# An attention turn written out in another order, with the identity matrix built by VectorE

## The chip, the cores and the metric

One core of a Trainium2 chip runs the whole program. The metric is the device time of one execution in microseconds, and a kernel is compared by the median of its runs. Names of engines here: TensorE (PE in the rows; PEld is its weight load), VectorE (DVE), ScalarE (ACT), GpSimd (POOL), and SyncE (SP), whose queue issues nearly all DMAs.

## What is computed

Attention with a random-feature kernel over 4 batches, 8 heads, 576 positions of 64 elements, with 128 features; its output goes through two MLPs (512 to 2048 to 512) on 2304 rows. Queries, keys, values are fp32; the MLP weights come in as fp64.

```python
def phi(x):
    proj = np.einsum('bhsd,df->bhsf', x, w_phi)
    proj = proj - np.max(np.abs(proj), axis=-1, keepdims=True)
    return np.concatenate([np.exp(proj), np.exp(-proj)], axis=-1)
q_p, k_p = (phi(q), phi(k))
kv = np.einsum('bhsf,bhsd->bhfd', k_p, v)
z = np.sum(k_p, axis=2)
num = np.einsum('bhsf,bhfd->bhsd', q_p, kv)
den = np.einsum('bhsf,bhf->bhs', q_p, z)[..., None] + 1e-06
return (num / den).astype(np.float32)
...
h = x @ w_in                      # first MLP
g = np.maximum(0.01 * h, h)
x = (g @ w_out).astype(np.float32)
...
h = x @ w_in                      # second MLP
sp = np.where(h > 20.0, h, np.log1p(np.exp(np.minimum(h, 20.0))))
out = ((h * np.tanh(sp)) @ w_out).astype(np.float32)
```

## The kernel before

The work is cut into 16 pairs (a batch and two heads). Of 576 positions, 512 are the main part (four blocks of 128) and 64 are left over; the leftovers of two neighbouring pairs are projected together, so `k_proj_left` comes in every other turn.

Nothing schedules the instructions: inside `manual_schedule` each engine runs them in the order in which the Python code issues them, and semaphores do the rest. `start()` prepares pairs 0 and 1. Then the loop over `attention(n)` runs n = 0 to 16, one **turn** each, with three pairs in hand: the sums and numerators of w = n, the projections of p = n + 1, the transposes of t = n + 2, and the loads of t + 1.

The steps of a turn are these. `transposes` turns keys and queries on TensorE with the identity matrix; `split` (L76 to L78) evicts them as a high part on ScalarE (`kth`, `qth`, `lh`) and a low part on VectorE (`ktl`, `qtl`, `ll`). `q_left` casts the leftover queries into place (L286). `q_proj` (four calls) and `k_proj` (two) project with three matmuls for each product (`three`, L81 to L83); `k_guard` subtracts the maximum from the keys' projections (`mx` L290, `kd` L291), while queries are copied by ScalarE (`qd`, L328), reduced over partitions by POOL (`qm`, L330, one call for each head) and guarded by VectorE in `q_guard` (L335). `exp` (L313) makes `qp` and `kp` for both signs. `kv(i, c)` sums key features times values for head h and sign a (c = 2h + a), `L353` copies the sums from PSUM, `nd` multiplies queries with them (L373, L365) and divides (L377 to L386), and `x_t` transposes the result into `X` one turn later (L395 to L399).

`Conv` turns fp64 weights into fp32: a unit is clamped (L147), shifted (L149), rescaled on ScalarE (L150), its sign and low bits taken (`e`, L156) and joined (`c`, L128); a unit that is kept in SBUF is then split by `split_w` into `wh` (ScalarE, L166) and `wl` (VectorE, L167). `conv0` has 10 units of the kind split and then 5 of the kind store, one for each of turns 1 to 15; each `step` finishes the unit opened a turn earlier and opens the next. Its data come through `Conv.load`, on SP's queue.

PSUM has four banks for the ring `a` (transposes, projections) and four for `b` (sums, numerators, x). After the turns, `moe(g)` runs the two MLPs; its first two steps already stand in turns 14 and 15. The identity comes from the library's `make_identity` (L194), a memset and a select on POOL. In turns 8 to 11, `window(0, ...)` splits a part of `X` behind the turn.

The order of a turn before, in its own lines:

```python
            if has_w:
                q_guard(w)
            if has_p:
                q_proj(p, 0)
                k_proj(p, 0)
                q_proj(p, 1)
            if has_w:
                if w:
                    kv(w, 0)
                q_exp(1)
            if has_p:
                q_proj(p, 2)
                k_proj(p, 1)
            if has_w:
                q_exp(-1)
            if has_p:
                q_proj(p, 3)
                if p % 2 == 0:
                    k_proj_left(p)
```

Of the kernel before, what the change touches and what calls it, by code (L numbers as in the profile page):

```python
# [24 lines left out]
def attention_two_mlps_kernel(  # L25
# [12 lines left out]
    nc = tc.nc  # L38
# [51 lines left out]
    class Conv:  # L90
# [5 lines left out]
        def __init__(self, which, units):  # L96
            self.which, self.units, self.at, self.loaded = which, units, 0, 0
            self.stage, self.open = {}, None
# [19 lines left out]
        def done(self):  # L118
            return self.at == len(self.units) and self.open is None

# [69 lines left out]

    with tc.manual_schedule():
        nc.scalar.preload_act_table_set("natural_log_exp_and_others")
        ident = ap.tile([P, P], F32, name="ident", bufs=1)
        make_identity(nc, ident)  # L194
        wbd = ap.tile([P, 2, F], F32, name="wbd", bufs=1)
        nc.vector.memset(wbd, 0.0)
        nc.vector.memset(two, 2.0)
# [20 lines left out]
        def load(i):  # L218
            b, p = divmod(i, NP)
# [8 lines left out]
            if i % 2 == 0:  # L228
# [9 lines left out]
            vm = s["vm"] = vmain[i % NV]  # L238
            nc.sync.dma_start(
                out=vm[:, :, 0:NM, :].rearrange("p h t d -> p h (t d)"),  # L240
                in_=v[b, h0:h0 + 2, 0:MAIN, :].rearrange("h (p t) d -> p h (t d)", t=NM),
            )
            vl = s["vl"] = vleft[i % NV]
            for r in range(2):
                nc.sync.dma_start(out=vl[r * LEFT:(r + 1) * LEFT, r, 0:D], in_=v[b, h0 + r, MAIN:S, :])
# [3 lines left out]
        load(0)  # L249
        load(1)  # L250
# [86 lines left out]
        def kv(i, c):  # L337
            s, l = st[i], lf[i // 2]
            h, a = divmod(c, 2)
            if c == 0:  # L340
                s["kvp"] = bank("b")
            o = s["kvp"][:, c * P:(c + 1) * P]

            for t in range(NM):
                nc.tensor.matmul(out=o, lhsT=s["kp"][a][:, h, t, :], rhs=s["vm"][:, h, t:NM + 1:NM - t, :],  # L345
                                 start=(c == 0 and t == 0), stop=False, skip_group_check=True)
            if c == 3:
                both = s["kvp"].rearrange("p (h a n) -> p h a n", h=2, a=2)
                for x in range(2):
                    nc.tensor.matmul(out=both[:, :, x, 0:D + 1], lhsT=l["lp"][x][:, i % 2, :], rhs=s["vl"],  # L350
                                     start=False, stop=(x == 1), skip_group_check=True)
                s["kv"] = ap.tile([P, 4, P], F32, tag="kv", name="kv", bufs=1)
                nc.scalar.activation(out=s["kv"], in_=s["kvp"].rearrange("p (c n) -> p c n", n=P), func=AF.Copy)  # L353

        def nd(i, c):
            s = st[i]
            t = bank("b")
            if c == 0:
                s["xn"] = ap.tile([P, NM, 2, D], F32, tag="xn", name="xn")
            if c == 2:  # L360

                g = t[:, 0:2 * (D + 1)].rearrange("p (c n) -> p c n", n=D + 1)
                kv_ = s["kv"].rearrange("p (h a) n -> p h a n", a=2)
                for a in range(2):
                    nc.tensor.matmul(out=g, lhsT=s["qp"][a].rearrange("p h n -> p (h n)")[:, MAIN:MAIN + P], rhs=kv_[:, :, a, 0:D + 1],  # L365
                                     start=(a == 0), stop=(a == 1))
                ng = 2
            else:
                g = t.rearrange("p (c n) -> p c n", n=P)
                for j, u in enumerate(range(2 * c, 2 * c + 2)):  # L370
                    for h in range(2):
                        for a in range(2):
                            nc.tensor.matmul(out=g[:, 2 * j + h, 0:D + 1], lhsT=s["qp"][a][:, h, Q_COL[h][u]:Q_COL[h][u] + P],  # L373
                                             rhs=s["kv"][:, 2 * h + a, 0:D + 1], start=(a == 0), stop=(a == 1))
                ng = 4
            den = ap.tile([P, 4], F32, tag="den", name="den")[:, 0:ng]
            nc.vector.tensor_scalar(out=den, in0=g[:, :, D], scalar1=1e-6, scalar2=None, op0=ALU.add)  # L377
            nc.vector.reciprocal(out=den, in_=den)
            if c == 2:
                s["xl"], s["lb"] = xleft[i % 2], t  # L380
                for h in range(2):
                    r = slice(h * LEFT, (h + 1) * LEFT)
                    nc.vector.tensor_scalar(out=s["xl"][r, h], in0=g[r, h, 0:D], scalar1=den[r, h:h + 1], scalar2=None,
                                            op0=ALU.mult)
            else:
                nc.vector.tensor_tensor(  # L386
                    out=s["xn"][:, 2 * c:2 * c + 2].rearrange("p a h d -> p (a h) d"), in0=g[:, :, 0:D],
                    in1=den.unsqueeze(2).to_broadcast([P, ng, D]), op=ALU.mult)

        def x_t(i):  # L390
# [6 lines left out]
            o = s["lb"][:, 2 * P:2 * P + LEFT]  # L397
# [4 lines left out]
        def k_exp(i):  # L402
            if i % 2 == 0:
                lf[i // 2]["lp"] = [exp(lf[i // 2]["kd"], "lp", sg) for sg in (1, -1)]
            st[i]["kp"] = [exp(st[i]["kd"], "kp", sg) for sg in (1, -1)]

        def start():
# [12 lines left out]
            kp_head(0, 1)  # L420
# [3 lines left out]
            k_proj_left(0)  # L424
            transposes(1, "k")
# [3 lines left out]
            kp_head(1, 0)  # L429
            kp_head(1, 1)  # L430
            kv(0, 0)
            kv(0, 1)
            load(2)

        def attention(n):
# [4 lines left out]

            def q_exp(sg):
                if sg == 1:
                    st[w]["qp"] = []
# [279 lines left out]
```

## Time and profile before

| what | value |
|---|---|
| median of 3 runs | 1033.09 us (1032.63 to 1036.21) |
| profiled execution, its own time | 1029.51 us |
| its span, first to last instruction | 1027.7 us |
| TensorE busy | 1001.1 us (97%) |
| VectorE, ScalarE, POOL busy | 753.2, 501.3, 72.6 us |
| chain of work that ended last | PE 92%, DVE 5%, issue 1%, ACT 1% |
| DMA | 72.84 MB, mean 71 GB/s |

The profile is of one execution; its own time is the span and 1.8 us around it, and 3.6 us below the median of the runs. Busy time adds up what instructions took. A matmul that follows another overlaps with it, so its row begins before the row ahead ends; the distance between two starts says how fast TensorE really goes. `x4` merges four neighbours, and a bracket at the end of a row gives the idle time just ahead on that engine and what ended it. A waiting instruction of an engine holds everything behind it on that engine.

### The profile page before, as it was taken

To read this page: it belongs to the slowest core of one execution; us is meant where nothing else is said; L and a number is where in the kernel's file an instruction comes from. 1 tells how busy PE (TensorE), PEld (TensorE's weight loads), DVE (VectorE), ACT (ScalarE), POOL (GpSimd) and SP (SyncE) were. 2 spreads that over 40 slices of the span, in tenths; PEclk is the share of its full clock that TensorE was granted. 3 is DMA by queue.
4 is the path that set the end of the run, shared out by engine and by line. 5 is a ranking of instruction groups with operands and counts; after the bars stand their busy time and mean duration, and the time that the engine had idled before them with its cause. 6 is when DMAs were issued, how large, how long until landed. Compare 5 with 4: busy or idle time off the path is not lost.

```text
span 1027.7 us, 14556 instructions
## 1 busy us (share of the span) xinstructions
PE 1001.1 (97%) x5544; PEld 871.2 (85%) x5544; DVE 753.2 (73%) x1389; ACT 501.3 (49%) x839; POOL 72.6 (7%) x38
## 2 busy tenths in 40 slices
PE   6999999999999999999999999999999999999998
PEld 5999988998888888998888888888888988888886
DVE  5888898876995666666533546978876888868976
ACT  4666666654554333343333445545544555545543
POOL 3322333220000000000000000000000000000000
PEclk9999999999999999999999999999999999999999
DMA  4333323313541344444311221000100100001001
GB/s 130 111 111 111 100 82 93 121 43 113 160 148 42 123 144 154 134 144 136 110 62 31 93 82 62 1 1 0 41 1 1 41 1 21 1 1 41 1 1 42
DMA packets 55494, 72.84 MB, mean 71 GB/s; under 512 B 10496, under 2 KB 39808, under 8 KB 55424
## 3 DMA queue, kind: packets, MB, share of 16 engines
q1 hardware_dynamic: 55264, 71.84, 21.6%
q8 instruction: 44, 0.72, 0.3%
q14 instruction: 26, 0.21, 0.1%
q10 hardware_dynamic: 160, 0.07, 0.0%
HBM read 57.48 MB, written 14.42 MB: 70 GB/s over the span
## 4 chain that ended last, share of the span: by engine, by line
PE 92%; DVE 5%; issue 1%; ACT 1%; POOL 0%; ACTq 0%; DVEq 0%; POOLq 0%
PE a L81 14%; PE a L82 14%; PE a L83 14%; PE b L82 13%; PE b L81 13%; PE b L83 13%; PE b L373 6%; PE b L345 4%; DVE qd L335 1%; PE a L266 1%; DVE kd L291 1%; DVE mx L290 1%; ACT kv L353 1%; PE b L395 1%; PE b L350 1%
## 5 line engine op out<-in xcount | busy, mean ns | idle before, releaser
L81 PE MATMUL a<-wh,wh 128*128 128x512 f32 (+1 forms) x640 | 235.6, 368 | 0.0
L82 PE MATMUL a<-wl,wh 128*128 128x512 f32 (+1 forms) x640 | 235.4, 368 | 0.0
L83 PE MATMUL a<-wh,wl 128*128 128x512 f32 (+1 forms) x640 | 235.4, 368 | 0.0
L81 PEld LDWEIGHTS a<-wh,wh 128*128 128x128 f32 x640 | 120.6, 188 | 20.2
L82 PEld LDWEIGHTS a<-wl,wh 128*128 128x128 f32 x640 | 120.7, 189 | 20.1
L83 PEld LDWEIGHTS a<-wh,wl 128*128 128x128 f32 x640 | 120.6, 188 | 20.0
L571 DVE TENSOR_TENSOR gl<-g,gh 128x512 fp32r<-128x512 f32 x72 | 49.9, 693 | 110.1 <-ACT gh L568 110.1
L82 PE MATMUL b<-gl,wh 128*128 128x512 f32 (+1 forms) x320 | 117.7, 368 | 0.0
L81 PE MATMUL b<-gh,wh 128*128 128x512 f32 (+1 forms) x320 | 117.7, 368 | 0.0
L83 PE MATMUL b<-gh,wl 128*128 128x512 f32 (+1 forms) x320 | 117.7, 368 | 0.0
L82 PE MATMUL b<-wl,gh 128*128 128x512 f32 x288 | 112.1, 389 | 0.0
L81 PE MATMUL b<-wh,gh 128*128 128x512 f32 x288 | 112.1, 389 | 0.0
L83 PE MATMUL b<-wh,gl 128*128 128x512 f32 x288 | 112.1, 389 | 0.0
L568 ACT ACTIVATE gh<-g 128x512 fp32r<-128x512 f32 x72 | 45.5, 632 | 115.9 <-PE b L83 109.4
L330 POOL PARTITION_ALL_REDUCE qm<-qd x32 | 71.9, 2249 | 140.7 <-DVE qd L335 122.1
L593 ACT ACTIVATE gh<-u 128x512 fp32r<-128x512 f32 x72 | 45.6, 633 | 70.6 <-PE b L82 63.9
L567 DVE TENSOR_TENSOR g<-g,a 128x512 f32<-128x512 f32 x72 | 49.4, 686 | 38.0 <-ACT g L564 35.2
L150 ACT ACTIVATE c<-c 128x512 f32<-128x512 f32 x64 | 40.3, 630 | 68.5 <-DVE c L147 68.3
L373 PE MATMUL b<-kv,qp 128*128 128x65 f32 x512 | 62.7, 276 | 7.5 <-ACT kv L353 7.5
L620 ACT ACTIVATE r<-e,two 128x512 f32<-128x512 f32 x72 | 51.7, 718 | 36.3 <-DVE e L605 36.3
L83 PEld LDWEIGHTS b<-gh,wl 128*128 128x128 f32 x320 | 60.3, 189 | 10.1
L81 PEld LDWEIGHTS b<-gh,wh 128*128 128x128 f32 x320 | 60.4, 189 | 10.0
(103 smaller groups left out, 1773.7 us busy)
## 6 DMA issues: line engine op xcount, KB each, us to landing
stage<-in_moe_w_in_dram SPq DMA_DIRECT2D x32, 512.0 KB, 3.6
stage<-in_moe_w_out_dram SPq DMA_DIRECT2D x32, 512.0 KB, 3.5
scr<-c SPq DMA_DIRECT2D x37, 256.0 KB, 2.0
wstage<-scr SPq DMA_DIRECT2D x32, 256.0 KB, 3.8
kn<-in_k_dram SPq DMA_DIRECT2D x16, 256.0 KB, 3.8
qn<-in_q_dram SPq DMA_DIRECT2D x16, 256.0 KB, 4.0
vmain<-in_v_dram SPq DMA_DIRECT2D x16, 256.0 KB, 3.2
out_dram<-X SPq DMA_DIRECT2D x16, 256.0 KB, 2.2
```

The source lines that it names most:

```text
L81: nc.tensor.matmul(out=o, lhsT=wh_, rhs=xh, start=start, stop=False)
L82: nc.tensor.matmul(out=o, lhsT=wh_, rhs=xl, start=False, stop=False)
L83: nc.tensor.matmul(out=o, lhsT=wl_, rhs=xh, start=False, stop=stop)
L150: nc.scalar.activation(out=c, in_=c, func=AF.Copy, scale=2.0 ** -112)
L330: nc.gpsimd.partition_all_reduce(s["qm"][:, h, :], s["qd"][:, h, :], P, bass_isa.ReduceOp.absmax)
L345: nc.tensor.matmul(out=o, lhsT=s["kp"][a][:, h, t, :], rhs=s["vm"][:, h, t:NM + 1:NM - t, :], start=(c == 0 and t == 0), stop=False, skip_ ...
L373: nc.tensor.matmul(out=g[:, 2 * j + h, 0:D + 1], lhsT=s["qp"][a][:, h, Q_COL[h][u]:Q_COL[h][u] + P], rhs=s["kv"][:, 2 * h + a, 0:D + 1], s ...
L567: nc.vector.tensor_tensor(out=g, in0=g, in1=h, op=ALU.max)
L568: nc.scalar.activation(out=hi, in_=g, func=AF.Copy)
L571: nc.vector.tensor_tensor(out=lo, in0=g, in1=hi.bitcast(F32), op=ALU.subtract)
L593: nc.scalar.activation(out=hi2, in_=u2, func=AF.Copy)
L620: nc.scalar.activation(out=r0, in_=e0, func=AF.Ln, bias=two)
```

## The change

The identity is built on VectorE by eight small instructions (`identity`): a running count 1 to 32 along a row, its 32 x 32 transpose, and four comparisons. `load` issues keys and queries at the head of a turn and returns a function that issues the values, which is called after the sums. A turn begins with all four query projections, then both query exponentials, then the key projections; the sums are made by sign (`kv(i, a)`, both heads and the leftovers), so that the exponential of the next pair's first sign stands between them; `q_guard(p)` stands in the turn that projected p. `x_t` comes ahead of the numerators. `nd` uses two PSUM banks instead of three, with six divisors in the second. `conv0.step` becomes `begin`, ahead of the transposes, and `join`, between the numerators; the low half `wl` of a unit follows at the next `begin`.

```diff
+        def begin(self):
+            self.load(1)
+            if self.rest is not None:
+                self.rest()
...
+            nc.vector.tensor_scalar(out=c, in0=hw.bitcast(F32), scalar1=F64_TOP, scalar2=-F64_TOP,
+                                    op0=ALU.min, op1=ALU.max)
+            nc.vector.tensor_scalar(out=lw, in0=lw, scalar1=29, scalar2=None, op0=ALU.logical_shift_right)
+            self.open = (u, kind, c, hw, lw)
+            return lambda: nc.scalar.activation(out=c, in_=c, func=AF.Copy, scale=2.0 ** -112)
+        def join(self):
...
+            nc.vector.scalar_tensor_tensor(out=e, in0=hw, scalar=-(1 << 31), in1=lw,
+                                           op0=ALU.bitwise_and, op1=ALU.bitwise_or)
+            self.load(1)
+            nc.vector.scalar_tensor_tensor(out=c.bitcast(I32), in0=c.bitcast(I32), scalar=3, in1=e,
+                                           op0=ALU.logical_shift_left, op1=ALU.bitwise_or)
+            if kind == "store":
...
+            else:
+                self.rest = split_w(self.which, u // 2, u % 2, c)
...
+    def identity(out):
+        Q = 32
+        one, row, col = (ap.tile([P, Q], F32, name=x, bufs=1) for x in ("one", "row", "col"))
+        nc.vector.memset(one, 1.0)
+        nc.vector.memset(out, 0.0)
+        nc.vector.tensor_tensor_scan(out=row, data0=one, data1=one, initial=0.0, op0=ALU.mult, op1=ALU.add)
+        nc.vector.transpose(out=col, in_=row)
+        for r in range(0, P, Q):
+            nc.vector.tensor_tensor(out=out[r:r + Q, r:r + Q], in0=row[r:r + Q], in1=col[r:r + Q], op=ALU.is_equal)
...
-        make_identity(nc, ident)
...
+        identity(ident)
...
-        def kv(i, c):
+        def kv(i, a):
...
+            for h in range(2):
+                for t in range(NM):
+                    nc.tensor.matmul(out=both[:, h, a, :], lhsT=s["kp"][a][:, h, t, :], rhs=s["vm"][:, h, t:NM + 1:NM - t, :],
+                                     start=(a == 0 and h == 0 and t == 0), stop=False, skip_group_check=True)
+            nc.tensor.matmul(out=both[:, :, a, 0:D + 1], lhsT=l["lp"][a][:, i % 2, :], rhs=s["vl"],
+                             start=False, stop=(a == 1), skip_group_check=True)
...
             kp_head(0, 0)
-            kp_head(0, 1)
             k_proj(0, 1)
...
             k_proj_left(0)
+            kp_head(1, 0)
             transposes(1, "k")
...
-            kp_head(1, 0)
+            kp_head(0, 1)
             kp_head(1, 1)
+            q_guard(0)
             kv(0, 0)
-            kv(0, 1)
-            load(2)
+            load(2)()
...
+            values = load(t + 1) if t + 1 < PAIRS else lambda: None
+            if has_p:
+                for c in range(4):
+                    q_proj(p, c)
             if has_w:
-                q_guard(w)
+                st[w]["qp"] = [exp(st[w]["qd"], "qp", sg) for sg in (1, -1)]
...
+                for c in range(2):
+                    k_proj(p, c)
+                if p % 2 == 0:
+                    k_proj_left(p)
...
                 if w:
                     kv(w, 0)
...
+                if has_p:
+                    k_exp(p, 0)
+                kv(w, 1)
+                kv_copy(w)
+            values()
             if has_p:
...
+                q_guard(p)
+            rebase = conv0.begin() if n >= CONV0 else lambda: None
             if has_t:
                 transposes(t)
                 q_left(t)
             elif has_w:
                 moe(n - (PAIRS - 2))
+            rebase()
             if has_p:
-                k_exp(p)
-            if has_w:
-                nd(w, 0)
+                k_exp(p, 1)
             if 0 <= w - 1:
                 x_t(w - 1)
             if has_w:
+                nd(w, 0)
+            conv0.join()
+            if has_w:
                 nd(w, 1)
-                nd(w, 2)
-            if t + 1 < PAIRS:
-                load(t + 1)
```

Where instructions stand, at the three places of which the prediction speaks. First TensorE from a turn's last sums to its end, before (`vmain`, `vleft` are the values, `kn`, `qn` keys and queries to be transposed, `xn` the divided result of the pair ahead):

```order
L345 MATMUL b<-vmain_89,kp 128x128 x12
L350 MATMUL b<-vleft_92,lp 128x2x65 x2
L266 MATMUL a<-ident,kn 128x128 x4
L266 MATMUL a<-ident,qn 128x128 x4
L373 MATMUL b<-kv,qp 128x65 x8
L395 MATMUL b<-ident,xn 128x128 x4
L398 MATMUL b<-fold,xleft_94 128x64
L373 MATMUL b<-kv,qp 128x65 x8
L365 MATMUL b<-kv,qp 128x130 x2
```

and now:

```order
L398 MATMUL b<-vmain_96,kp 128x128 x8
L400 MATMUL b<-vleft_99,lp 128x2x65
L398 MATMUL b<-vmain_96,kp 128x128 x8
L400 MATMUL b<-vleft_99,lp 128x2x65
L318 MATMUL a<-ident,kn 128x128 x4
L318 MATMUL a<-ident,qn 128x128 x4
L445 MATMUL b<-ident,xn 128x128 x4
L448 MATMUL b<-fold,xleft_101 128x64
L419 MATMUL b<-kv,qp 128x65 x16
L425 MATMUL b<-kv,qp 128x130 x2
```

The transposes of `xn` and the leftovers' fold moved ahead of the first numerators, which are now in one run with the second; the sums of a pair stand together.

Second, ScalarE from the head of a turn, before (`qd` the query copies, `wh` and `c` of the conversion, `kv` the copy of the sums):

```order
L328 ACTIVATE qd<-a 128x320
L328 ACTIVATE qd<-a 128x256
L313 ACTIVATE qp<-qd 128x1152
L328 ACTIVATE qd<-a 128x256
L313 ACTIVATE qp<-qd 128x1152
L328 ACTIVATE qd<-a 128x320
L166 ACTIVATE wh_975<-c 128x512
L150 ACTIVATE c<-c 128x512
L353 ACTIVATE kv<-b 128x512
L77 ACTIVATE kth<-a 128x512
L77 ACTIVATE qth<-a 128x2x256
```

and now, from the end of one turn into the next:

```order
L137 ACTIVATE c<-c 128x512
L365 ACTIVATE kp<-kd 128x1024
L446 ACTIVATE X<-b 128x512
L202 ACTIVATE wh_564<-c 128x512
L380 ACTIVATE qd<-a 128x320
L380 ACTIVATE qd<-a 128x256 x2
L380 ACTIVATE qd<-a 128x320
L365 ACTIVATE qp<-qd 128x1152 x2
L365 ACTIVATE lp<-kdl 128x256
L365 ACTIVATE kp<-kd 128x1024
L406 ACTIVATE kv<-b 128x512
```

The copy `wh` of a conversion unit moved from the middle of the next turn to the end of its own, directly ahead of the next turn's query copies, and the rescaling `c` from ahead of the `kv` copy to behind the evictions.

Third, SP's queue from the loads of pair 3 to those of pair 4, before (`stage` is a conversion unit's data):

```order
L224 DMA kn<-in_k_dram 128x2x256
L224 DMA qn<-in_q_dram 128x2x256
L239 DMA vmain_88<-in_v_dram 128x2x256
L245 DMA vleft_91<-in_v_dram 64x64 x2
L115 DMA stage<-in_moe_w_in_dram 128x4x256
L115 DMA stage<-in_moe_w_out_dram 128x1024
L115 DMA stage<-in_moe_w_in_dram 128x4x256
L224 DMA kn<-in_k_dram 128x2x256
L224 DMA qn<-in_q_dram 128x2x256
L234 DMA kl<-in_k_dram 64x2x64 x2
L234 DMA ql<-in_q_dram 64x2x64 x2
```

and now:

```order
L272 DMA kn<-in_k_dram 128x2x256
L272 DMA qn<-in_q_dram 128x2x256
L289 DMA vmain_95<-in_v_dram 128x2x256
L295 DMA vleft_98<-in_v_dram 64x64 x2
L272 DMA kn<-in_k_dram 128x2x256
L272 DMA qn<-in_q_dram 128x2x256
L282 DMA kl<-in_k_dram 64x2x64 x2
L282 DMA ql<-in_q_dram 64x2x64 x2
L289 DMA vmain_96<-in_v_dram 128x2x256
L295 DMA vleft_99<-in_v_dram 64x64 x2
L114 DMA stage<-in_moe_w_in_dram 128x4x256
L114 DMA stage<-in_moe_w_out_dram 128x1024
```

The first two `stage` loads moved from ahead of all of pair 4's loads to behind its last values.

## Rows read from the trace of the kernel before

**Rows 1.** The page's part 1: busy us (share of the span) xinstructions.

```profile
PE 1001.1 (97%) x5544; PEld 871.2 (85%) x5544; DVE 753.2 (73%) x1389; ACT 501.3 (49%) x839; POOL 72.6 (7%) x38
```

**Rows 2.** Stretches: their length, then busy us of each engine, clock, DMA.

```profile
113.00:127.20 14.20, 13.40 (x115) 12.93 (x114) 12.06 (x27) 9.34 (x16) 4.28 (x2) 1.00 0.35 113
127.20:140.90 13.70, 13.06 (x114) 12.82 (x113) 12.41 (x26) 9.52 (x16) 4.76 (x2) 1.00 0.30 92
450.00:1027.00 577.00, 573.15 (x2641) 478.89 (x2639) 410.09 (x687) 265.12 (x435) 0.00 (x0) 1.00 0.11 38
```

**Rows 3.** TensorE's waits to 260 us: waiter, releaser, total us, times, longest.

```profile
PE a L266 <- POOL ident masks.py:199: 9.2, 1, 9.2
PE b L373 <- ACT kv L353: 7.5, 12, 1.2
```

**Rows 4.** Timeline, TensorE, turns 7 and 8: start, us, instruction, idle before.

```profile
113.02 0.39 PE L81 MATMUL a<-qth,wbh 128*128 128x320 f32 x1
117.58 0.35 PE L81 MATMUL a<-wbh,lh 128*128 128x256 f32 x1 [0.38 <-DVE kd L291]
122.60 2.00 PE L373 MATMUL b<-kv,qp 128*128 128x65 f32 x16 [0.42 <-ACT kv L353]
127.25 0.39 PE L81 MATMUL a<-qth,wbh 128*128 128x320 f32 x1
136.28 2.00 PE L373 MATMUL b<-kv,qp 128*128 128x65 f32 x16 [0.64 <-ACT kv L353]
140.94 0.39 PE L81 MATMUL a<-qth,wbh 128*128 128x320 f32 x1
```

**Rows 5.** Timeline of TensorE: first query matmul of turns 1 and 14.

```profile
29.91 0.39 PE L81 MATMUL a<-qth,wbh 128*128 128x320 f32 x1
...
213.19 0.39 PE L81 MATMUL a<-qth,wbh 128*128 128x320 f32 x1
```

**Rows 6.** Timeline of POOL and TensorE to the start of turn 0.

```profile
8.86 0.28 POOL masks.py:199 TENSOR_SCALAR_AFFINE_SELECT ident<-ident 128x128 f32<-128x128 f32 x1 [7.93 <-issue]
9.20 1.11 PE L266 MATMUL a<-ident,kn 128*128 128x128 f32 x4 [9.20 <-POOL ident masks.py:199]
13.10 0.39 PE L81 MATMUL a<-qth,wbh 128*128 128x320 f32 x1 [0.34 <-DVE qtl L286]
15.03 4.30 POOL L330 PARTITION_ALL_REDUCE qm<-qd  x2 [5.89 <-ACT qd L328]
16.42 0.62 PE L266 MATMUL a<-ident,qn 128*128 128x128 f32 x4
19.52 0.39 PE L81 MATMUL a<-qth,wbh 128*128 128x320 f32 x1 [0.70 <-DVE qtl L286]
```

**Rows 7.** SP's queue; DMA issues to 4.6 us, KB, us to landing.

```profile
3.31 1.25 SPq L234 DMA_DIRECT2D ql<-in_q_dram  x2
...
kn<-in_k_dram SPq DMA_DIRECT2D x1, 256.0 KB, 2.7
...
ql<-in_q_dram SPq DMA_DIRECT2D x2, 32.0 KB, 2.1
```

**Rows 8.** Timeline of SP's queue, and DMA issues from 26.0 to 26.5 us.

```profile
24.62 0.37 SPq L239 DMA_DIRECT2D vmain<-in_v_dram  x1
26.24 0.58 SPq L115 DMA_DIRECT2D stage<-in_moe_w_in_dram  x1
...
stage<-in_moe_w_in_dram SPq DMA_DIRECT2D x1, 512.0 KB, 3.8
```

**Rows 9.** Timeline of POOL and VectorE in turns 7 and 8.

```profile
118.92 2.14 POOL L330 PARTITION_ALL_REDUCE qm<-qd  x1 [0.69 <-ACT qd L328]
120.68 0.65 DVE L147 TENSOR_SCALAR c<-stage 128x512 f32<-128x512 f32 x1
133.14 2.62 POOL L330 PARTITION_ALL_REDUCE qm<-qd  x1 [0.69 <-ACT qd L328]
133.50 1.52 DVE L147 TENSOR_SCALAR c<-stage 128x512 f32<-128x512 f32 x1
```

More of the change, by code (lines that the diff above doesn't have):

```diff
@@ L97, in __init__ @@
             self.which, self.units, self.at, self.loaded = which, units, 0, 0
-            self.stage, self.open = {}, None
+            self.stage, self.open, self.rest = {}, None, None
         def load(self, ahead):
@@ L237, in load, with values @@
                         )
[L238 to L245, printed above, removed]
+            def values():
+                vm = s["vm"] = vmain[i % NV]
+                nc.sync.dma_start(
+                    out=vm[:, :, 0:NM, :].rearrange("p h t d -> p h (t d)"),
+                    in_=v[b, h0:h0 + 2, 0:MAIN, :].rearrange("h (p t) d -> p h (t d)", t=NM),
+                )
+                vl = s["vl"] = vleft[i % NV]
+                for r in range(2):
+                    nc.sync.dma_start(out=vl[r * LEFT:(r + 1) * LEFT, r, 0:D], in_=v[b, h0 + r, MAIN:S, :])
+            return values
         for r in range(2):
             nc.scalar.dma_start(out=wbd[r * D:(r + 1) * D, r, :], in_=w_phi)
-        load(0)
-        load(1)
+        load(0)()
+        load(1)()
         wbh = ap.tile([P, 2 * F], F32R, name="wbh", bufs=1)
@@ L335, in q_guard, with kv_copy @@
             nc.vector.tensor_tensor(out=s["qd"], in0=s["qd"], in1=s["qm"], op=ALU.subtract)
-        def kv(i, c):
+        def kv(i, a):
             s, l = st[i], lf[i // 2]
-            h, a = divmod(c, 2)
-            if c == 0:
+            if a == 0:
                 s["kvp"] = bank("b")
[L342 to L353, printed above, removed]
+            both = s["kvp"].rearrange("p (h a n) -> p h a n", h=2, a=2)
+            for h in range(2):
[4 more added lines that the diff above has]
+                             start=False, stop=(a == 1), skip_group_check=True)
+        def kv_copy(i):
+            s = st[i]
+            s["kv"] = ap.tile([P, 4, P], F32, tag="kv", name="kv", bufs=1)
+            nc.scalar.activation(out=s["kv"], in_=s["kvp"].rearrange("p (c n) -> p c n", n=P), func=AF.Copy)
         def nd(i, c):
@@ L454, in attention @@
                     kv(w, 0)
-                q_exp(1)
-            if has_p:
-                q_proj(p, 2)
-                k_proj(p, 1)
-            if has_w:
-                q_exp(-1)
-            if has_p:
-                q_proj(p, 3)
-                if p % 2 == 0:
-                    k_proj_left(p)
-            if n >= CONV0 and not conv0.done():
-                conv0.step()
-            if has_w:
-                for c in range(1 if w else 2, 4):
-                    kv(w, c)
+                if has_p:
[3 more added lines that the diff above has]
+            values()
+            if has_p:
+                q_guard(p)
+            rebase = conv0.begin() if n >= CONV0 else lambda: None
             if has_t:
```

71 lines of the change are left out of this document (37 added, 34 removed).

## The prediction

> **What bounds the kernel now.** I went from the page to stages, then to single turns. The page first: TensorE is busy for 1001.1 of 1027.7 us [rows 1], so at most 26.6 us of the span are open to any reordering; what can move must be TensorE idle. By stage, the last 577 us hold only 3.9 us of it [rows 2]; the diff leaves that part's instruction order alone, so it can only start earlier. The idle time is at the start and in the attention turns, and the waits say for what: 9.2 us for the identity matrix that POOL builds, 7.5 us in 12 waits for ScalarE's copy of the sums `kv` [rows 3], and a smaller wait at the leftover key projection.
>
> Next, two neighbouring turns by starts of TensorE [rows 4]. Turn 7 lasts from 113.02 to 127.25, 14.23 us. The leftover key projection would have followed the last query projection at 117.04, but starts at 117.58: 0.54 lost to `kd`. The numerator's first matmul would follow the transposes at 122.02 and starts at 122.60: 0.58 lost to `kv`. Turn 8 lasts 13.69 us; its numerator starts at 136.28 instead of 135.48: 0.80 lost. Without these waits the turns are 13.11 and 12.89 us. Turns 1 to 13 run from 29.91 to 213.19 [rows 5], 183.3 us; seven of the long and six of the short kind without waits would be 169.1, so **14.2 us** is what the turns can give. The busy rows give less: the two windows show 0.80 and 0.64 us idle [rows 2], over thirteen turns 9.4. I take the starts, as a matmul after a wait has its fill counted as busy. The Trainium skill (Trainium Kernel Development and Optimization, Performance Expectations) also calls matmul busy time a bad metric because matmuls are pipelined; by the busy rows the sum below would be 8.6 us, by the starts 13.4, and which is right the changed profile will tell.
>
> **The change part by part.**
>
> *Identity.* POOL's select ends at 9.14 and TensorE begins at 9.20 [rows 6]; the keys `kn` were issued at 0.72 and take 2.7 us [rows 7], so they lie there from 3.4 on. VectorE's eight new small instructions appear in no row; bounded by a 0.06 us memset and the 0.42 us of a 128x256 operation they are 0.5 to 3.4 us, and I take 1.2, as most are as small as the memsets. Begun at about 1.1 they end at 2.3, before the keys; the other memsets that they push back end by 4.4, before anything needs them. The next limit is then the leftover queries: the last `ql` is issued at 3.93 and takes 2.1 [rows 7], so the leftover transposes end at about 6.1 instead of 11.2. From there to the first query projection the chain of splits and casts takes 1.9 us, so 8.0 instead of 13.10 [rows 6]: 5.1 gained. In `start` one half of the key exponentials now waits for the second `kd` ahead of the eviction of pair 1's keys: about 0.5 lost. Turn 0 begins near 15.0 instead of 19.52: **4.5 gained**. POOL loads code ahead of its reductions; before, this was hidden in the 5.9 us between the select and the first reduction [rows 6], now it may take what the select waited for (7.9 us), ending near 9, when the first reduction is due at 9.9. If both waits add up it ends at 13.8 and turn 0 gets some 2.5 longer.
>
> *Turn order.* TensorE now does four q, two k (and the leftover one), both signs of the sums, then the transposes, then x's transposes, then the numerators. The copy of `kv` (0.58 us) lies behind 0.87 us of transposes and 0.61 of x's, so the wait of 0.58 to 0.80 goes. The wait for `kd` goes too: the leftover projection's PSUM bank is now one that ScalarE's third query copy frees, about 1 us before it is due. In turn 0 there is no x to cover the copy: 0.3 lost. At the end the last x's transposes stand directly behind the last numerator and wait for its division: 0.3 lost.
>
> *Guard in the same turn.* The q guard (1.36 us) moves on VectorE ahead of conversion and of the splits of `kt` and `qt`, and waits for POOL. From a turn's start: first query copy at 0.80, second done at 1.55, two reductions of 2.14 [rows 9] to 5.95, guard to 7.3, low half of the weight 0.61, two conversion steps 0.91, splits 1.2 to 1.5, casts 0.3: 10.6. The next turn's first query matmul, which waits for the casts, is due at 12.9: 2.3 us of cover. If POOL were 2.3 us later, each further delay would land on TensorE.
>
> *Conversion in two pieces.* Before, three steps ran beside POOL's second reduction and were stretched: the clamp takes 1.52 us there and 0.65 elsewhere, the reduction 2.62 instead of 2.14 [rows 9]. Now POOL is done before the first piece starts. But the rounding copy `wh` now stands on ScalarE after the second piece and ahead of the next turn's query copies, and so closes a loop in turns 1 to 10, its steps reckoned from the starts of like instructions in turns 7 and 8: `wh` 0.56 and two query copies 0.75, two reductions 4.30, guard 1.27, weight 0.61, conversion 0.91, splits 1.37, casts and x 0.52, first division 0.75, second piece 1.36, handovers 0.25: 12.65, against TensorE's 12.89 to 13.11. It fits by 0.3 us. A first query copy that is late by more than 0.35 holds the k projection, which needs its bank. Three turns with a window split (0.6 us) in the same place may lose 0.2 each: **0.6 lost**.
>
> *Loads.* Keys and queries now go out at the head of a turn, values after the sums; both have a turn in hand. SP works in order, though: the first two `stage` loads now stand behind the values of pair 4, and these wait for turn 1's sums, 7.5 us into the turn. From value load to stage load SP needs 1.6 us (24.62 to 26.24), landing 3.8 [rows 8]: the weight arrives at 12.9, where VectorE wants it at 7.3. Behind that wait are the splits and casts: they end at 15.3 in place of 10.6, so turn 2, due at 13.0, starts 2.4 late; then its query copies stand behind `wh`, which comes at 17.7, and the k projection is 1.7 late: **4.1 lost once**. A landing of 3.5 to 4.4 makes it 3.7 to 4.7. Later stage loads have a turn in hand.
>
> *Divisions.* Two instead of three: two short VectorE steps less, 0.4 us a turn, all hidden.
>
> **Sum.** 4.5 + 14.2 - 0.3 - 0.3 - 0.6 - 4.1 = 13.4 us. The profiled execution took 1029.5 us, so 1016.1 by it; the median of the runs is 3.6 higher, 1033.1, and becomes **1019.7**. With 2.8 to 5.1 at the start, 9.4 to 14.9 in the turns and 3.7 to 4.7 lost once, the gain is 6.5 to 15.5: 1017.5 to 1026.5, and 1014 if the turns also catch up what turn 1 loses.
>
> **Rivals.** (1) *The conversion loop binds.* If its handovers cost 0.05 to 0.1 us more at each of its some twenty steps, it lasts 13.6 to 14.0, and nine or ten turns lose 0.6 to 1.0 each, 6 to 9 us: 1026 to 1029. For it: only 0.3 us of room. Against: POOL's stretch goes.
> (2) *The array stays at half pace.* Four transposes take 1.11 us at 9.20 and 0.62 at 16.42 [rows 6]. If TensorE, begun at 3.4 and then waiting for `ql`, reaches full pace no earlier than before, about 12.4, the start's projections end there instead of at 15.5: 3.1 gained less 0.5, so 2.6 instead of 4.5: 1021.6. The Trainium skill (TensorE: Matmul & The Clock Gate, What's actually happening) says that the default is throttled and activity releases it, which speaks for this rival; no row of the trace before has an early start with a gap.
> (3) *Slower: reductions and conversion still collide.* If the loop keeps the stretch of [rows 9], with reductions of 2.62 and the three conversion steps together 2.4 longer, it lasts 16.0 us, 2.0 more than turns 2 to 10 last now (126.4 in nine): 18 lost there, 3.5 in turns 1 and 2, 4.2 gained at the start and 4.3 in turns 11 to 13: 1033.1 + 13 = 1046. It decides against the change from a loop of about 14.3 us on. Against it: the guard waits for both reductions, and conversion stands behind the guard.
> (4) *The first load is not late*, because TensorE's sums end earlier than reckoned or the wait hides: 4 us more, 1015.6.
>
> **Chances.** Forecast 0.55, (1) 0.20, (2) 0.12, (4) 0.08, (3) 0.05. What a measurement can tell here is about 0.5%, 5.2 us, so up to 1027.9 counts as faster: all of forecast, (2) and (4) but 0.02 each for what I overlooked, and 0.14 of (1): faster 0.85, same 0.10, slower 0.05. The range for 8 in 10 leaves out (3), the upper end of (1) and little below (4): 1013 to 1028.
>
> **What would show it.** TensorE's first matmul at about 3.5 us; turn 0 at 15.0. Turns of 12.9 to 13.1 us from the third on, with no wait for `kv` or `kd`. One gap of some 4 us around turns 1 and 2, with VectorE waiting for `stage`. All reductions at 2.14 us and the clamp at 0.65. I am wrong if turns settle at 13.6 or more with TensorE waiting for ScalarE's query copies, if POOL's first reduction starts after 12, or if anything in the last 577 us takes a different time.

## The result and the profile after

The changed kernel takes 1015.62 us (median of 4 runs, 1014.77 to 1017.45), the kernel before 1032.86 beside it (4 runs): ratio 0.9834, 95% interval 0.9805 to 0.9862, so 17.2 us faster. The forecast was 1019.7 in 1013 to 1028. The profiled executions differ by less than the medians: 1029.51 against 1014.77, 14.7 us; their spans by 14.95 (1027.72 to 1012.77).

The page of the changed kernel, parts 1 and 4. It answers to [rows 1]: TensorE lacked 26.6 us before and lacks 13.8 now.

```profile
PE 999.0 (99%) x5544; PEld 871.9 (86%) x5544; DVE 732.5 (72%) x1365; ACT 500.5 (49%) x839; POOL 68.7 (7%) x36
...
PE 97%; DVE 1%; DMA 1%; SPq 0%; ACT 0%; issue 0%; DVEq 0%; ACTq 0%
```

TensorE's waits to 260 us (waiter, releaser, total us, times, longest), against [rows 3]:

```profile
PE a L318 <- DVE vleft L253: 3.6, 1, 3.6
PE a L80 <- DVE qtl L338: 2.5, 2, 1.9
PE a L80 <- ACT qd L380: 1.4, 1, 1.4
PE b L445 <- DVE xn L430: 0.9, 1, 0.9
PE b L419 <- ACT kv L406: 0.7, 1, 0.7
PE a L328 <- DMA ql<-in_q_dram: 0.4, 1, 0.4
```

The 9.2 us for the identity are 3.6. The first row names a memset, but what the code needs there is `kn` (landing 2.7 us after its issue, as in [rows 7]); a wait for several things is put down to the one that came last by the profile, and in stage_early below the same wait is put down to `kn`. Of twelve waits for `kv` one is left, in turn 0. Two are new: 1.9 of the 2.5 for `qtl`, and 1.4 for a query copy, once each. They are the late first weight. The wait for the last division (`xn`) grew from 0.2 to 0.9.

Turns 7 and 8 as two windows (length, then busy us of TensorE, its weight loads, VectorE, ScalarE, POOL, clock, DMA) and the last 577 us, against [rows 2]:

```profile
107.28:120.24 12.96, 12.96 (x116) 12.96 (x115) 10.91 (x26) 9.29 (x16) 4.26 (x2) 1.00 0.41 114
120.24:133.06 12.82, 12.82 (x115) 12.82 (x114) 10.58 (x25) 8.95 (x15) 4.26 (x2) 1.00 0.34 107
435.00:1012.00 577.00, 573.62 (x2645) 479.37 (x2644) 410.58 (x688) 265.46 (x436) 0.00 (x0) 1.00 0.11 38
```

An ordinary turn has no idle TensorE left, and the last part is as it was. The timeline of the same turn 7 (start, us, instruction, idle before), against [rows 4, 9]:

```profile
107.28 0.39 PE L80 MATMUL a<-qth,wbh 128*128 128x320 f32 x1
...
107.54 0.63 ACT L202 ACTIVATE wh<-c 128x512 fp32r<-128x512 f32 x1 [1.89 <-DVE c L149]
...
108.08 1.51 ACT L380 ACTIVATE qd<-a 128x320 f32<-128x320 f32 x4
...
108.89 4.26 POOL L382 PARTITION_ALL_REDUCE qm<-qd  x2 [8.56 <-ACT qd L380]
...
113.39 1.35 DVE L387 TENSOR_TENSOR qd<-qd,qm 128x1152 f32<-128x1152 f32 x1
...
114.77 0.60 PE L318 MATMUL a<-ident,kn 128*128 128x128 f32 x4
115.03 0.60 ACT L406 ACTIVATE kv<-b 128x512 f32<-128x512 f32 x1
...
115.26 0.42 DVE L133 TENSOR_SCALAR c<-stage 128x512 f32<-128x512 f32 x1
...
116.25 3.74 PE L419 MATMUL b<-kv,qp 128*128 128x65 f32 x32
116.48 0.64 ACT L137 ACTIVATE c<-c 128x512 f32<-128x512 f32 x1
```

The two reductions take 4.26 together, the clamp 0.42 (1.52 and 0.65 before): it starts 2.1 us after POOL has ended. The copy of `kv` ends at 115.63, 0.62 ahead of the numerators; the rescaling `c` (L137) comes behind it.

The start, against [rows 6]:

```profile
1.70 0.77 DVE L236 TENSOR_TENSOR ident<-row,col 32x32 f32<-32x32 f32 x4
...
3.60 1.09 PE L318 MATMUL a<-ident,kn 128*128 128x128 f32 x4 [3.60 <-DVE vleft L253]
...
6.27 0.45 PE L328 MATMUL a<-ident,ql 128*128 128x128 f32 x1 [0.40 <-DMA ql<-in_q_dram]
...
7.84 0.61 PE L80 MATMUL a<-qth,wbh 128*128 128x320 f32 x1
...
10.13 4.26 POOL L382 PARTITION_ALL_REDUCE qm<-qd  x2 [9.71 <-ACT qd L380]
...
10.52 0.31 PE L80 MATMUL a<-qth,wbh 128*128 128x320 f32 x1
...
15.00 0.39 PE L80 MATMUL a<-qth,wbh 128*128 128x320 f32 x1 [0.63 <-DVE qtl L338]
```

And the gap around turns 1 and 2:

```profile
35.24 0.58 SPq L114 DMA_DIRECT2D stage<-in_moe_w_in_dram  x1
...
39.02 0.43 DVE L133 TENSOR_SCALAR c<-stage 128x512 f32<-128x512 f32 x1 [5.42 <-DMA stage<-in_moe_w_in_dram]
...
41.23 0.39 PE L80 MATMUL a<-qth,wbh 128*128 128x320 f32 x1 [1.88 <-DVE qtl L338]
...
43.48 0.63 ACT L202 ACTIVATE wh<-c 128x512 fp32r<-128x512 f32 x1 [1.64 <-DVE c L149]
...
44.49 0.38 PE L80 MATMUL a<-wbh,kth 128*128 128x256 f32 x1 [1.44 <-ACT qd L380]
```

Starts of the first query matmul cut both traces into the prediction's steps:

| step | before | after | gain | forecast |
|---|---|---|---|---|
| turn 0 begins at | 19.52 | 15.00 | 4.52 | 4.5 |
| turn 0 | 10.38 | 11.14 | -0.76 | -0.3 |
| turns 1 and 2 | 27.29 | 29.59 | -2.30 | part of the next |
| turns 1 to 13 | 183.28 | 172.07 | 11.21 | 9.5 (14.2 - 0.6 - 4.1) |
| turn 14 to the end | 814.53 | 814.56 | 0.0 | -0.3 |

### The profile page after: what moved, and what is told of

It reads as the page before. It is cut to its first block, busy times and chain, and to the rows that moved or that the text cites. A ratio compares the mean times of both kernels' runs of the same rounds, so it can differ in the third digit from the quotient of the medians.

```text
span 1012.8 us, 14523 instructions
## 1 busy us (share of the span) xinstructions
PE 999.0 (99%) x5544; PEld 871.9 (86%) x5544; DVE 732.5 (72%) x1365; ACT 500.5 (49%) x839; POOL 68.7 (7%) x36
## 4 chain that ended last, share of the span: by engine, by line
PE 97%; DVE 1%; DMA 1%; SPq 0%; ACT 0%; issue 0%; DVEq 0%; ACTq 0%
PE a L80 15%; PE a L81 15%; PE a L82 15%; PE b L81 13%; PE b L80 13%; PE b L82 13%; PE b L398 5%; PE b L419 5%; PE a L318 1%; PE b L425 1%; PE b L400 1%; PE b L445 1%; DMA stage<-in_moe_w_in_dram 0%; PE b L448 0%; DMA ql<-in_q_dram 0%
## 5 line engine op out<-in xcount | busy, mean ns | idle before, releaser
L382 POOL PARTITION_ALL_REDUCE qm<-qd x32 | 68.5, 2188 | 135.1 <-ACT qd L380 135.1
L81 PEld LDWEIGHTS b<-gl,wh 128*128 128x128 f32 x320 | 60.4, 189 | 10.0
L631 ACT ACTIVATE e<-a 128x512 f32<-128x512 f32 x72 | 42.9, 596 | 47.8 <-PE a L82 27.0
```

The costliest lines, as they stand in the source:

```text
L81: nc.tensor.matmul(out=o, lhsT=wh_, rhs=xl, start=False, stop=False)
L382: nc.gpsimd.partition_all_reduce(s["qm"][:, h, :], s["qd"][:, h, :], P, bass_isa.ReduceOp.absmax)
L631: nc.scalar.activation(out=e0, in_=h0, func=AF.Exp)
```

## The experiments

In the expectations, theory A is the prediction's: the `kv` waits go because transposes and x's transposes now lie between the sums and the numerators. Theory B is that they go because the rescaling no longer stands ahead of the copy on ScalarE. Spans and turn lengths below are those of each profiled execution, cut as in the table.

### Each half of the change alone

**ident_only**: the kernel before with the new identity.

```diff
...
-        ident = ap.tile([P, P], F32, name="ident", bufs=1)
-        make_identity(nc, ident)
         wbd = ap.tile([P, 2, F], F32, name="wbd", bufs=1)
         nc.vector.memset(wbd, 0.0)
+        ident = ap.tile([P, P], F32, name="ident", bufs=1)
+        identity(ident)
```

> The kernel before with the identity built by VectorE and nothing else. Theory: the first transposes start at 3.6 us, the start's chain is limited by ql, turn 0 starts at 14.5 to 15.0 instead of 19.52, and nothing gives it back: 4.5 to 5.0 us faster. Rival (half pace lasts as long as before): 2.6 us or less. Rival (POOL's code load delays the first reduction): turn 0 longer by over 1 us, 2 to 3 us faster.

1024.69 us (1024.27 to 1026.77), ratio 0.9942 (0.9922 to 0.9962). Turn 0 begins at 14.74 and all turns are as before; the span is 1022.63, 5.1 shorter. Two of TensorE's waits to 260 us in this kernel:

```profile
PE b L383 <- ACT kv L363: 7.5, 12, 1.2
PE a L80 <- DVE kd L301: 3.7, 7, 0.9
```

The start's gain is the identity's alone, and the 11.2 us of waits in these two rows are left for the order to remove.

**order_only**: the changed kernel with the diff above undone, so that only the order is new.

> The changed kernel with the library's identity on POOL again. Theory: the two parts add up. Turn 0 starts at 19.5 to 20.0, the turns are as in the changed kernel, 4.5 to 5.0 us slower than it and some 10 us faster than before. Rival (the parts hang together, for instance through POOL or the loads at the start): 3 us or less, or over 6 us, slower than the changed kernel.

1021.77 us (1020.55 to 1023.45), ratio 0.9916 (0.9893 to 0.9938). Turn 0 begins at 19.62, turns 3 to 8 last 12.96 and 12.82 as with both halves, the span is 8.9 shorter. 5.1 and 8.9 are 14.0 of the 14.95; the missing 0.9 lies for the most part in turns 0 and 1 (11.77 and 15.51 against 11.14 and 15.09). The halves add up to within that.

### Which part of the order removes the kv wait

**x_late**: x's transposes back behind the first numerators.

```diff
-            if 0 <= w - 1:
-                x_t(w - 1)
             if has_w:
                 nd(w, 0)
+            if 0 <= w - 1:
+                x_t(w - 1)
             conv0.join()
```

> The changed kernel with x's transposes behind the first numerators again, as before. Theory A, as predicted (x's transposes cover the copy of the sums): the waits for kv come back, 0.5 to 0.8 us in each of some 13 turns, 6 to 10 us slower than the changed kernel. Theory B (the copy now starts at once, because the rescaling no longer stands ahead of it on ScalarE; it ends 0.9 us after the sums, and the transposes alone cover it): no wait over 0.15 us in turns 3 to 13, within 1 us of the changed kernel.

1015.47 us (1014.99 to 1016.46), ratio 0.985 (0.9832 to 0.9868): no difference. Between 60 and 180 us TensorE has no wait at all, and turns 3 to 8 last 13.05 and 12.77. In turn 7 of x_late:

```profile
115.60 0.60 ACT L406 ACTIVATE kv<-b 128x512 f32<-128x512 f32 x1
...
116.25 2.00 PE L419 MATMUL b<-kv,qp 128*128 128x65 f32 x16
...
117.05 0.64 ACT L137 ACTIVATE c<-c 128x512 f32<-128x512 f32 x1
```

The copy ends at 116.20, just before the numerators, with the pair's own transposes as its only cover. A's second half, x's transposes, isn't needed. It even costs a little elsewhere: in x_late the first division of turn 7 comes 10.44 us into the turn instead of 10.96, and turns 9 to 11, which last 13.16, 13.03 and 13.18 in the changed kernel, last 13.05, 12.78 and 13.07. So the 0.2 that each of them loses beside a window's split (see wh_twice) hangs on x standing first. It doesn't show in the total, since turn 1 is 0.46 longer here.

**rescale_ahead**: the converse, x's transposes left in their new place and the rescaling back ahead of the copy.

```diff
                 kv(w, 1)
-                kv_copy(w)
...
-            rebase = conv0.begin() if n >= CONV0 else lambda: None
+            if n >= CONV0:
+                conv0.begin()()
+            if has_w:
+                kv_copy(w)
...
-            rebase()
```

> The changed kernel, with the rescaling of `c` put back where it stood before the change on ScalarE: ahead of the copy of `kv`, both of them ahead of the evictions of the transposes. Theory B (the waits for `kv` went because the rescaling no longer stands ahead of the copy): in the changed kernel's turn 7 the clamp ends at 115.68, so the rescaling would run to about 116.3 and the copy to 116.9, where the numerators now start at 116.25. They should wait 0.6 to 0.8 us in each of turns 1 to 13, with x's transposes still ahead of them: turns of 13.5 to 13.7 instead of 12.9, 8 to 10 us more, 1022 to 1026 us. Theory A (the transposes and x's transposes cover the copy wherever it stands): no wait, 1015 to 1016.

1029.71 us (10 runs, 1028.21 to 1037.11), ratio 0.9993 (0.9974 to 1.0012): the whole gain is gone, more than either theory gave. Turns 3 to 8 are 13.67 and 13.44, as B said, but turn 1 alone lasted 24.25: the copy there also waited for the late weight (5.6 us). So this run couldn't carry the verdict alone, and the next one takes that load away.

**rescale_early**: rescale_ahead with the first load at the end of `start`, as in stage_early below.

> The rescaling ahead of the copy of `kv`, as in rescale_ahead, with the first `stage` load issued at the end of `start`, as in stage_early. rescale_ahead's turns 3 to 8 lasted 13.67 and 13.44 (0.66 more than in the changed kernel), but turn 1 alone lasted 24.25, because the copy also waited for the late first load. If that is the whole of it, turn 1 is now about 13.6, every turn of 1 to 13 costs 0.6 to 0.7, and the total is 8 to 9 above the 1010.5 of stage_early: 1018 to 1021 us. If the extra of turn 1 has another cause (the order on ScalarE itself, or the low clock in two stretches), turn 1 stays over 16 and the total over 1024.

1018.60 us (1018.20 to 1019.46), ratio 0.9878 (0.9859 to 0.9897). Turn 1 lasts 13.05, turns 3 to 8 13.66 and 13.45; turns 1 to 13 together are 8.1 longer than in stage_early, and the median 8.1 above its 1010.5. Its turn 7, which begins at 106.60:

```profile
114.60 0.42 DVE L133 TENSOR_SCALAR c<-stage 128x512 f32<-128x512 f32 x1
...
115.06 0.63 ACT L137 ACTIVATE c<-c 128x512 f32<-128x512 f32 x1 [0.78 <-DVE c L133]
...
115.59 0.58 ACT L406 ACTIVATE kv<-b 128x512 f32<-128x512 f32 x1
...
116.22 3.79 PE L419 MATMUL b<-kv,qp 128*128 128x65 f32 x32 [0.47 <-ACT kv L406]
```

TensorE's wait for the copy from 50 to 180 us (total, times, longest), where the changed kernel has none:

```profile
PE b L419 <- ACT kv L406: 4.6, 9, 0.9
```

The numerators start 9.62 us into the turn instead of 8.97. Clamp, rescaling and copy are one chain there, and both covers together don't hide it. Theory B is shown for the changed kernel: the place of one 0.63 us rescaling on ScalarE is worth 0.65 us a turn.

In the kernel before, a second step stood ahead of the copy, and it moved too: `wh` (L166). ScalarE there, in turn 7 and (last row) turn 8:

```profile
120.79 0.63 ACT L166 ACTIVATE wh<-c 128x512 fp32r<-128x512 f32 x1 [1.97 <-DVE c L128]
121.43 0.63 ACT L150 ACTIVATE c<-c 128x512 f32<-128x512 f32 x1
121.97 0.58 ACT L353 ACTIVATE kv<-b 128x512 f32<-128x512 f32 x1
...
135.12 0.63 ACT L150 ACTIVATE c<-c 128x512 f32<-128x512 f32 x1 [0.87 <-DVE c L147]
```

The sums end at 121.30 and 134.55, `wh` at 121.42 and 134.25. So without the rescaling the copy would have ended near 122.0 and 135.2, and the numerators were due at 122.02 and 135.48: by these rows, as an estimate, the rescaling alone makes the wait there as well, and `wh` doesn't. No run moved the rescaling alone in the kernel before.

The other 11.1 us between the medians of rescale_ahead and rescale_early are the late load ahead of the copy and the low clock that came with it (rescale_ahead's profiled execution, 1036.29 us, has three stretches at half clock; more on that below).

### The late first load, and turn 0

**stage_early**: one line at the end of `start`, so that the first weight's load stands ahead of turn 0's loads on SP.

```diff
             load(2)()
+            conv0.load(1)
```

> The changed kernel with the first two stage loads issued in the start, behind the loads of pair 2. Theory: VectorE finds the first unit's data in turn 1, turns 1 and 2 last 13.1 and 12.9 us instead of 15.1 and 14.5, 3.5 to 4 us faster than the changed kernel. Rival (another wait takes its place, the loads of pair 3 come too late or the conversion loop holds turn 2 anyway): less than 2 us faster.

1010.50 us (1010.43 to 1011.56), ratio 0.9803 (0.9786 to 0.9821), faster than both kernels. Turns 1 and 2 are 12.97 and 12.82; turns 1 to 13 last 168.29, 3.8 less than in the changed kernel. Another 0.65 is an earlier start, which the edit doesn't explain (below).

**exp_behind**: the exponential of the next pair's first sign behind the copy.

```diff
-                if has_p:
-                    k_exp(p, 0)
                 kv(w, 1)
                 kv_copy(w)
...
             if has_p:
+                k_exp(p, 0)
                 k_exp(p, 1)
```

> The changed kernel, with the exponential of the next pair's first sign behind the copy of `kv` instead of ahead of it. If turn 0's wait of 0.72 us for `kv` is that exponential's (it waits for `kd` to 20.50 and runs to 21.56, the copy behind it), the wait goes and the total falls by 0.5 to 0.8; the steady turns keep 12.96 and 12.82, since the exponential there ends before the sums do (114.93 against 114.94 in turn 7): 1014.0 to 1015 beside 1014.8. If the place between the sums also carries something in the steady turns, other waits appear there (the last copies of x, `wh`, or the query copies late) and the turns get 0.1 us or more longer: over 1016.

1014.96 us (1014.06 to 1016.46), ratio 0.9841 (0.9822 to 0.9859). Turn 0 lasts 10.14 instead of 11.14 and the wait for `kv` is gone from the list; 0.4 comes back in turn 1, where the first load is issued only 0.64 earlier (34.60 against 35.24), though the turn begins 1.0 earlier. Turns 3 to 8 keep 12.96 and 12.82. So turn 0's loss was this exponential, which stands ahead of the copy and waits there for `kd`.

**early_and_behind**: both edits, with the diffs of stage_early and exp_behind.

> The changed kernel with both mends: the first `stage` load at the end of `start` and the exponential of the next pair's first sign behind the copy of `kv`. If the two are independent, turn 0 lasts 10.1 instead of 11.1, turns 1 and 2 last 13.0 and 12.8, and the span is 1 us below that of stage_early with the same start (stage_early's start had full clock 1.8 us earlier, worth 0.6): 1009.3 to 1010.5 us. If the exponential's new place only moves the wait, 1010.5 to 1011.5.

1010.23 us (5 runs, 1009.21 to 1010.99), ratio 0.9797 (0.9778 to 0.9817), the lowest median tried. Turns 0, 1 and 2 last 10.14, 12.98 and 12.82, the span is 1007.31 against 1008.36: the two add up in the trace, while their medians can't be told apart. What TensorE still waits for to 260 us:

```profile
PE a L318 <- DVE vleft L253: 3.5, 1, 3.5
PE b L445 <- DVE xn L430: 0.9, 1, 0.9
PE a L80 <- DVE qtl L338: 0.8, 2, 0.6
PE a L328 <- DMA ql<-in_q_dram: 0.5, 1, 0.5
```

### The guard, and the room in the conversion loop

**guard_late**: the query guard back at the head of the next turn (and pair 0's out of `start`).

```diff
...
+            if has_w:
+                q_guard(w)
             if has_p:
                 for c in range(4):
...
-            if has_p:
-                q_guard(p)
```

> The changed kernel, with the query guard back at the head of the next turn, so that it stands ahead of the key guards there and the two query exponentials wait for it. If only the order of ScalarE and of the sums gives the gain, the turns stay at 12.9 to 13.0 (the exponentials start 0.8 us later, and what follows them on ScalarE, the exponential of the keys, has 1.9 us of idle time ahead of it): 1014.5 to 1016. If the guard's place is part of the gain, because VectorE's conversion then starts while POOL still reduces or the key guards come late, the clamp takes over 1 us, waits for `kd` or `kv` come back, and the turns are 13.2 or longer: 1019 and up.

1016.52 us (1014.56 to 1019.48), ratio 0.9857 (0.9833 to 0.9881). Turns 3 to 8 are 12.96 and 12.82 to the hundredth: in ordinary turns the guard's place is worth nothing. That is so although VectorE's conversion again runs beside POOL's reductions there: the clamp takes 0.56 or 0.66 in these turns instead of 0.42, and in every other one `wl` takes 1.37 instead of 0.68. So ending that overlap, which the prediction counted in the change's favour, gained no time in these turns. The profiled execution, 1019.48, had turns 0 and 1 of 12.52 and 17.13 with low clock in them; its runs spread over 5 us, so they say nothing finer on the total.

**wh_twice**: in `join`, the copy `wh` of a unit issued a second time.

```diff
                 self.rest = split_w(self.which, u // 2, u % 2, c)
+                hi = W[self.which, u // 2][0][:, u % 2].rearrange("p k f -> p (k f)")
+                nc.scalar.activation(out=hi, in_=c, func=AF.Copy)
```

> The changed kernel, with the rounding copy `wh` of each of the ten units of the kind split done twice, 0.56 to 0.63 us more on ScalarE directly ahead of the query copies, the result the same. By the prediction's loop (12.65 us, now 13.2) turns 2 to 10 would be 13.2 to 13.3 each: 3 to 4 us more. By the changed kernel's own rows there is about 0.5 us of slack ahead of the first division (VectorE idle 0.47), so the reductions' delay mostly disappears and only the key projection waits for its bank, 0.1 to 0.2 us a turn: 1 to 2 us more. If the loop never was near binding, 0 to 0.5 more; if every handover counts, 0.6 a turn, 6 us.

1021.61 us (1020.25 to 1023.08), ratio 0.9904 (0.9885 to 0.9923), 6.0 above the changed kernel. Its turn 7:

```profile
111.31 0.39 PE L80 MATMUL a<-qth,wbh 128*128 128x320 f32 x1
...
111.57 0.63 ACT L204 ACTIVATE wh<-c 128x512 fp32r<-128x512 f32 x1 [1.96 <-DVE c L149]
...
112.77 1.30 ACT L382 ACTIVATE qd<-a 128x320 f32<-128x320 f32 x4
...
113.24 0.39 PE L80 MATMUL a<-wbh,kth 128*128 128x256 f32 x1
```

From `wh` to the first query copy it is 1.20 instead of 0.54, so the second copy costs 0.66. Turns 3 to 8 are 13.32 and 13.18, 13.25 on average, so if the loop sets them, it lasts 12.59 without the second copy. The prediction's sum for the loop was 12.65. Each turn is 0.36 longer than in the changed kernel, so the room is 0.30 of the 0.66; what exceeds it is paid. In turns 9 to 11, where a window's split lies in the loop, wh_twice lasts 13.83, 13.69, 13.84 against 13.16, 13.03, 13.18: the full 0.66 to 0.67 more, so there the loop binds in the changed kernel already. My reading of the rows, 0.1 to 0.2 a turn, was wrong: VectorE's idle 0.47 ahead of the first division was not all slack. Of the span's 6.7 more, turns 3 to 8 and 9 to 11 make 2.2 and 2.0; turn 2 makes 2.3 (16.77 against 14.49), where a stretch of low clock fell too.

## Why the prediction was right, and where it was off

The forecast gain of 13.4 us measured 14.7 by the profiled executions and 17.2 by the medians. The start, the late load and the room in the conversion loop were right in their causes; the reason given for the largest part, the `kv` waits, was not.

- **Start, 4.5.** Measured 4.52, with the first matmul at 3.60, the first query projection at 7.84 (8.0) and turn 0 at 15.00. The identity's last comparison ended at 2.47 (2.3); its like rows in stage_early run from 1.07 to 2.46, 1.4 us against the estimate of 1.2. The first reduction at 10.13 (9.9) shows no added wait for POOL's code. That 4.5 was hit to 0.02 is luck: with the same instructions at the start, turn 0 begins between 14.26 and 15.79 in the runs above.
- **Turns, 14.2.** Without the late load (stage_early) turns 1 to 13 gained 15.0. The windows' 0.6 was 0.64 (turns 9 to 11 are 0.20 to 0.22 above their like). So the turns gained 1.4 more than summed: they settled at 12.96 and 12.82, not 13.11 and 12.89; where these 0.15 and 0.07 come from wasn't sought. The 14.2 was more than the waits: 1.12 in seven turns and 0.80 in six make 12.6. The rest came in because turns 9 to 12 of the kernel before, with a window's split, lasted 14.83 and 14.21, 2.3 together above their like, while its turns 1 and 2 were 0.6 below theirs; the prediction doesn't name this. The starts were the right reading and the busy rows too low: they would have given 9.4. The Trainium skill (Trainium Kernel Development and Optimization, Performance Expectations) calls matmul busy time a bad metric for how close a kernel is to roofline, because matmuls are pipelined; here, too, it misled, with 9.4 against the 15.0 measured.
- **Why the kv wait goes.** This step named the wrong part: "The copy of `kv` (0.58 us) lies behind 0.87 us of transposes and 0.61 of x's, so the wait of 0.58 to 0.80 goes." In x_late it goes without x's, in rescale_early it comes back with both covers in place. What decides is that the rescaling, chained to the clamp, left the place ahead of the copy. The size came out right only because both moves are in the change: that is luck.
- **The kd wait.** It is gone from the list, as forecast. It stays in ident_only (3.7 us in 7) and is in no list of a run with the new order. That a freed PSUM bank is the reason was only read from the code; no run isolated it.
- **Turn 0, -0.3.** Measured -0.76: I put it down to the missing cover of x, but it is the exponential ahead of the copy: with that moved (exp_behind) the wait is gone and turn 0 lasts 10.14, still with no x to cover the copy.
- **First load, -4.1.** Measured 3.8, with the links in the order forecast: clamp late, turn 2 1.9 late, k projection 1.4 late. Stage_early settles it.
- **End, -0.3.** The forecast wait for the last division is there (0.9 us), but from turn 14 on nothing was lost. The fold of the last pair ends 0.45 later after turn 14's start than before, and the rest is 0.42 shorter; what shortened it was not sought.
- **From the profiled execution to the median.** The terms gave 13.4 and the profiled executions 14.7. The forecast's other 2.8 us of error come from adding the 3.6 by which before's median lay above its profile to the changed kernel too; there it is 0.85.
- **Rivals.** (1) fell in ordinary turns, by the 0.30 us of room that wh_twice measured; it is true of the three turns with window splits. (2) fell: query matmuls take 0.31 at 10.52. The Trainium skill (TensorE: Matmul & The Clock Gate, What's actually happening) says the default state is throttled and activity releases it; the durations agree (1.09 for four transposes at 3.60, 0.60 at 11.32), but the pace doubled between 7.84 and 10.52, in spite of the gap for `ql`. (3) fell: reductions 2.13 each, clamp 0.42 (forecast 0.65). (4) fell: the load was late.
- **Slips in the sums.** By the prediction's own terms the gain runs from 6.3 to 15.1 (it says 6.5 to 15.5), rival (1)'s loop from 13.65 to 14.65 (13.6 to 14.0), and the chances for "faster" make 0.83 (0.85). None of them moves the forecast.

## What to carry to other kernels

Where several engines' copies feed one matmul, look at what stands ahead of the copy in its engine's own queue, and what that waits for, before counting cover on the matmul engine: moving one 0.63 us step was worth 0.65 us in each turn, the added cover nothing that showed in the total. When loads are moved in an in-order queue, follow the first use of every load issued behind them; here one line gave back 3.8 us. To know the room of a loop that is not yet binding, lengthen it by a known step: the turn's length then shows what the loop alone takes.

## What was not expected of the hardware

*The clock fell behind the gap.* In five of the seven profiled kernels that have the late load and the new order, the granted clock was 0.50 (1.2 GHz) for a stretch shortly behind the gap, the wait around turns 1 and 2 that the late load makes. Order_only, windows before, in and behind it (columns as above; TensorE's wait for `qtl` ended at 46.90):

```profile
43.00:46.00 3.00, 1.60 (x14) 1.41 (x13) 1.31 (x4) 0.85 (x3) 0.00 (x0) 1.00 0.72 276
46.50:49.50 3.00, 2.60 (x11) 2.63 (x12) 2.76 (x12) 1.36 (x3) 0.00 (x0) 0.50 0.02 4
50.00:53.00 3.00, 2.87 (x25) 2.84 (x25) 2.08 (x5) 3.00 (x6) 2.53 (x2) 1.00 0.95 324
```

The third number from the end is the clock. What it cost isn't the same everywhere: in order_only and exp_behind turn 2, where it fell, lasted 14.49 and 14.52 as in the changed kernel (14.49), and the wait of 1.4 us for the query copy is missing from their lists, so the slow matmuls seem to have filled it. Guard_late and rescale_ahead also show a clock of 0.54 from 25.0 to 32.4, ahead of the gap, so the gap isn't the only place where it falls.

The changed kernel's profiled execution was spared, but two of its four runs have a mean clock of 0.997 and take 1016.4 and 1017.5 us, against 1014.8 for the two at 1.0; neither of the two was profiled. All 13 runs of the three kernels with the early load have 0.999 or 1.0. So the late load costs its 3.8 us and goes with some 2 more in some executions; that the gap is what lowers the clock isn't shown. One run of ident_only, without the late load, has 0.997 too (1026.8 against 1024.3 to 1024.9), and the runs of the kernel before also spread (1029.4 to 1030.3 at 0.999 or 1.0, 1032.0 to 1032.9 at 0.995 to 0.997); none of those slower ones was profiled, and where their clock fell stays open.

*The pace at the start rises at a varying time.* The first query matmul took 0.61 at 7.84 in the changed kernel; in stage_early, with the same instructions ahead of it:

```profile
7.93 0.39 PE L80 MATMUL a<-qth,wbh 128*128 128x320 f32 x1
...
14.35 0.39 PE L80 MATMUL a<-qth,wbh 128*128 128x320 f32 x1 [0.63 <-DVE qtl L338]
```

Full pace came before the query projections, and turn 0 began at 14.35 instead of 15.00. This is read from the durations: the clock column shows 1.00 in both traces from 3 us on, also where matmuls take twice as long. Starts among these kernels with the new identity lie between 14.26 and 15.79; a difference of half a microsecond there can't be put down to an edit.

*A clamp of 128 x 512 on VectorE* takes 0.42 with POOL idle, against 0.65 and 1.52 where a reduction of POOL ran partly or wholly beside it [rows 9]; the reduction took 2.62 there instead of 2.13. Neither waited the other out there: both got longer. In guard_late only VectorE's steps did (clamp 0.56 or 0.66); the two reductions kept their 4.26.
